# First layer of the third last token group by seven products too, weight sums in the q and k staging tiles, sums added in place in PSUM

## The chip, the cores and the metric

The kernel runs on one core of a Trainium2 chip. The metric is the device time of one execution in microseconds. A profiled execution also gives its span, from its first to its last instruction, which is a little shorter than its time. Engines: PE multiplies matrices (PEld loads its weights), DVE and ACT do elementwise work, POOL issues loads and masks, SP issues stores. PSUM has eight banks of 512 fp32 columns; a matmul's result lands in one of them.

## The reference

Causal attention over 8 batches, 8 heads, 576 tokens of 64 dimensions with 16 extra "beacon" keys in front, then a two-layer MLP with a quick gelu on all 4608 tokens:

```python
scores = scale * np.matmul(q, k_all.transpose(0, 1, 3, 2))     # k_all: 16 beacons, then k
scores = np.where(causal, -1000000000.0, scores)
a = np.exp(scores - scores.max(-1, keepdims=True)); a /= a.sum(-1, keepdims=True) + 1e-09
x = np.matmul(a, v_all).transpose(0, 2, 1, 3).reshape(4608, 512)
h = x @ w_in                                                   # 512 x 2048
g = h * (1.0 / (1.0 + np.exp(-1.702 * h)))
return g @ w_out                                               # 2048 x 512
```

## The kernel before

**Attention** goes by 16 sets (a batch and four heads each). For a set, q and k are loaded into staging tiles (qn, kn, three of each, set s in number s % 3), transposed by DVE (L435), multiplied into score chunks (`qk0` to `qk54`, L464, shape 32x128), put through exp on ACT (L475) and masked on POOL (L496). DVE adds the columns for the normaliser (`zadd`, L514). The value products (`av`, L551, shape 128x32) have two halves of the normaliser per set (`av14.2.0` is set 14, normaliser, half 0) and three others; DVE turns and inverts the normaliser (`z1`, `z2`: L563, L570, L574) and writes the normed result to xT (`norm`, L586), 512 rows of the MLP's input by 2304 columns that are used in turn.

**The MLP** goes by ten token groups: two of 256 tokens, then eight of 512 (groups 2 to 9). Its weights w1t (first layer) and w2t lie in SBUF in fp16.

*First layer.* In groups 0 to 7 it is direct (L610): 16 tiles of 128 features, four 128x512 products each, then a gelu on ACT (L631). In groups 8 and 9 (`FAST`, L752) it uses seven products in place of eight on 2x2 blocks (Strassen and Winograd). Four sums of weight quarters are made once by DVE (`e_ws`, L755), four sums of token quarters per group (`e_xs`, L778). Then come four tiles, i = 0 to 3, of seven products each (L813); each product is four 128x256 matmuls. The sums of products are built in PSUM, in four banks a, b, e, f per tile: product 1 goes to a; ACT copies a to b (`seedb`, L823); product 2 is added in a, and ACT takes the gelu of a; product 6 is added in b, and ACT copies b to e (`seede`); product 7 goes to f, and ACT copies it to SBUF (`keep7`, L828). Product 5 is added in e; DVE adds the kept product 7 to it and writes the sum to SBUF (`sum22`, L831), and ACT takes the gelu from there. Product 3 is then added in e, for a third gelu. Product 4 is added in b; DVE adds product 7 (`sum21`), again into SBUF, for the fourth gelu (L837). The weight sums lie in a tile of the E pool (which otherwise holds exp's results) and in bkf, the token sums in another tile of that pool, and the kept and summed tiles in all six q and k staging tiles.

*Second layer.* Groups 2 to 9 use seven products as well (`products`, L1056; L724 on PE): DVE makes 16 sums of gelu results per group (`s`, L675), and a chain of one ACT copy (`half`, L735) and seven DVE joins (`join`, L740) builds four output quarters, which SP stores (L747).

**Order.** Every engine's order is written out: `ORDER` lists operation numbers, in the order in which the program makes the operations. `Plan.run` goes through these lists with planned durations to fix in which PSUM bank each tile opens and in what order instructions are emitted. Four lower banks (`ring`) are free for tiles all the time. The four upper banks hold the score chunk until the last exp, and from then on any tile may open there. A seeded tile (b or e) may only open in a bank that was fully written before and is closed. A bank is closed by the last reader named in `closers`: a by its gelu, f by `keep7`, b by `sum21`, e by its last gelu; a value tile by its z1 or norms; a product tile of the second layer by its half or join.

PE's list from the last but one score chunk to the first product of group 8, with names for numbers (`m1.7.6`: group 7, feature tile 6; `m2.6.5.4`: second layer of group 6, product 5, from feature tile 4; `f8.0.1`: group 8, tile 0, product 1):

```
qk53 m2.6.4.2 m2.6.7.4 m2.6.7.6 m2.6.5.0 m2.6.5.2 m2.6.4.4 qk54 m1.7.6 m2.6.5.4 m2.6.5.6 m2.6.4.6 m1.7.10 m1.7.1
av14.2.1 av14.2.0 m1.7.8 m2.6.3.4 m1.7.2 m1.7.9 m2.6.3.6 m1.7.13 m1.7.14 m1.7.15 m1.7.0 m1.7.3 m1.7.11 m1.7.4
m1.7.7 m2.7.5.0 m1.7.5 m1.7.12 av14.1.1 av15.2.1 av15.2.0 av14.0.0 av14.0.1 (16 of group 7's second layer)
av15.1.1 av15.0.0 av15.0.1 m2.7.2.6 f8.0.1
```

The lines that the change touches are those of `Plan.run` (L150), `ring_tile`, `e_qk`, L752 to L842, and `fast` and the loops behind it in the kernel's last third. The functions:

Of the kernel before, what the change touches and what calls it, by code (L numbers as in the profile page):

```python
# [32 lines left out]
        978, 1000, 992, 982, 974, 998, 990, 984, 988, 980, 1002, 986, 1256, 1156, 1113, 1111, 1115, 1159, 1025, 1020,  # L33
        1026, 1021, 1259, 1022, 1027, 1023, 1031, 1028, 1032, 1265, 1164, 1162, 1166, 1033, 1034, 1287, 1036, 1041,
        1054, 1055, 1037, 1289, 1042, 1038, 1039, 1047, 1048, 1043, 1292, 1192, 1049, 1050, 1044, 1180, 1170, 1275,
        1278, 1172, 1056, 1176, 1174, 1057, 1190, 1196, 1198, 1168, 1178, 1182, 1184, 1194, 1243, 1186, 1188, 1285,
        1301, 1304, 1281, 1283, 1227, 1237, 1244, 1216, 1238, 1217, 1218, 1221, 1232, 1245, 1222, 1219, 1223, 1228,
        1246, 1311, 1307, 1309, 1224, 1321, 1233, 1229, 1337, 1230, 1234, 1239, 1235, 1325, 1240, 1323, 1327, 1329,
        1341, 1330, 1339, 1343, 1333, 1250, 1251, 1353, 1252, 1346, 1253, 1345, 1359, 1422, 1357, 1355, 1369, 1349,
        1406, 1412, 1401, 1402, 1361, 1423, 1362, 1413, 1365, 1417, 1407, 1371, 1373, 1418, 1375, 1408, 1377, 1414,  # L40
        1403, 1378, 1428, 1381, 1429, 1451, 1445, 1404, 1409, 1419, 1415, 1467, 1461, 1447, 1430, 1431, 1465, 1424,
        1449, 1435, 1463, 1436, 1470, 1469, 1437, 1454, 1420, 1453, 1473, 1499, 1493, 1425, 1438, 1457, 1477, 1497,
        1546, 1495, 1479, 1481, 1483, 1502, 1501, 1485, 1552, 1536, 1547, 1505, 1525, 1526, 1489, 1486, 1541, 1537,
        1527, 1530, 1531, 1548, 1532, 1528, 1538, 1542, 1553, 1549, 1533, 1539, 1543, 1544, 1554, 1555, 1559, 1560,
        1561, 1562,
# [8 lines left out]
        836, 846, 830, 848, 850, 842, 1084, 879, 1087, 1090, 1099, 1097, 1118, 1121, 1147, 1150, 977, 995, 979, 997,  # L54
        993, 973, 975, 983, 991, 999, 989, 1001, 981, 1003, 985, 987, 1257, 1260, 1024, 1266, 1269, 1288, 1290, 1293,
        1181, 1171, 1177, 1175, 1173, 1191, 1179, 1169, 1185, 1197, 1183, 1193, 1195, 1189, 1187, 1199, 1220, 1322,
        1326, 1338, 1324, 1328, 1342, 1340, 1344, 1332, 1336, 1334, 1354, 1360, 1348, 1356, 1352, 1350, 1358, 1364,
        1370, 1366, 1368, 1372, 1374, 1376, 1380, 1382, 1384, 1452, 1405, 1446, 1468, 1462, 1448, 1466, 1464, 1450,
        1476, 1472, 1460, 1474, 1500, 1494, 1456, 1458, 1478, 1498, 1496, 1482, 1484, 1508, 1480, 1506, 1504, 1488,
        1490, 1492, 1529,  # L60
# [13 lines left out]
        945, 941, 943, 1081, 956, 957, 958, 871, 1082, 1094, 1095, 959, 872, 873, 867, 859, 961, 962, 964, 965, 860,  # L74
        863, 1262, 1143, 861, 874, 862, 868, 864, 967, 865, 971, 866, 969, 884, 869, 870, 1101, 1144, 890, 1145,
        1102, 895, 1103, 1104, 900, 906, 1109, 907, 1110, 913, 1106, 1107, 1152, 1153, 1004, 1154, 1005, 1155, 1264,
# [26 lines left out]
    ],  # L103
    "SP": [
        0, 2, 4, 5, 6, 7, 83, 84, 85, 86, 88, 89, 90, 91, 181, 93, 94, 95, 96, 187, 217, 223, 348, 364, 371, 377,
        544, 560, 567, 573, 689, 705, 712, 718, 885, 901, 908, 914, 1030, 1046, 1053, 1059, 1226, 1242, 1249, 1255,
        1411, 1427, 1434, 1440, 1535, 1551, 1558, 1564,
    ],
}
# [1204 lines left out]
```

## Time and profile before

| | |
|---|---|
| median of 3 runs | 326.32 us (326.07 to 326.36) |
| profiled execution, its time | 325.29 us |
| its span | 323.6 us |
| granted PE clock, mean | 0.998 |
| PE waits for others, whole span | 8.4 us, none after 92.1 us |
| first direct product of group 7 | 238.07 us |
| last exp | starts 238.23 us |
| first of the seven products (group 8) | 265.5 us |
| last products on PE | from 317.49 us, 16 of them |

In a row of a timeline stand the start, the length, the engine, line, operation, operands and count; a bracket gives the idle time of the engine before it and what ended that. In a row of groups, the busy time and the mean length of one in ns follow the bar. Lengths of neighbours overlap, since an instruction starts while the one before it is still draining: the distance of two starts is what an engine spends on one. The chain of work that ended last has PE in 83% of the span.

### The profile page before, as it was taken

What the parts mean: (1) busy time and instruction counts of PE and PEld (TensorE: products, weight loads), DVE (VectorE), ACT (ScalarE), POOL (GpSimd) and SP (SyncE); (2) the same over time, 40 slices, a digit from 0 to 9 for tenths busy, and PEclk for the clock granted to TensorE, in tenths of its full rate; (3) what the DMA queues carried; (4) which work ended last, traced back from release to release, by engine and by line L of the source; (5) the groups of instructions that cost most, each with busy time, mean ns of one, the idle gap of its engine ahead of it and who ended that gap; (6) DMA issues with size and microseconds to landing.
All of it is one profiled execution on the core that took longest, in us unless ns stands there. A gap on an engine that the chain in (4) does not pass through costs nothing.

```text
span 323.6 us, 10241 instructions
## 1 busy us (share of the span) xinstructions
PE 310.6 (96%) x4460; PEld 223.6 (69%) x4460; DVE 253.2 (78%) x508; ACT 213.7 (66%) x260; POOL 114.1 (35%) x178
## 2 busy tenths in 40 slices
PE   6589999999999999999999999999999999999994
PEld 6467765544775467745878878647765688888884
DVE  4837788777987989986998879858757788854865
ACT  1685687678767586679757696768664606576840
POOL 8775488190319312951068109500230000000000
PEclk9999999999999999999999999999999999999999
DMA  7999999293424921593019909800100101100203
GB/s 126 162 201 210 206 184 187 48 118 105 104 69 68 180 54 34 67 190 68 2 38 162 158 2 101 180 2 5 34 28 6 67 2 67 65 2 33 100 3 130
DMA packets 58222, 28.85 MB, mean 89 GB/s; under 512 B 41280, under 2 KB 53568, under 8 KB 58176
## 3 DMA queue, kind: packets, MB, share of 16 engines
q0 software_dynamic: 47552, 18.49, 48.3%
q1 hardware_dynamic: 10560, 9.69, 9.2%
q8 instruction: 35, 0.57, 0.7%
q14 instruction: 11, 0.09, 0.1%
q10 hardware_dynamic: 64, 0.01, 0.0%
HBM read 37.22 MB, written 9.44 MB: 144 GB/s over the span
## 4 chain that ended last, share of the span: by engine, by line
PE 83%; DMA 6%; ACT 3%; POOL 3%; DVE 3%; issue 1%; DVEq 0%; ACTq 0%; POOLq 0%
PE u L724 28%; PE u L610 27%; PE u L551 9%; PE s L464 8%; PE u L813 8%; PE u L655 4%; DMA w<-in_moe_w_out_dram 3%; DMA w<-in_moe_w_in_dram 2%; ACT E L475 2%; DVE osb L740 1%; DVE sA L675 1%; POOL vb L395 1%; POOL w L401 0%; ACT L631 0%; POOL kn L379 0%
## 5 line engine op out<-in xcount | busy, mean ns | idle before, releaser
L475 ACT ACTIVATE E<-s 128x2048 f16<-128x2048 f32 (+5 forms) x66 | 98.9, 1515 | 42.6 <-PE s L464 42.1
L610 PE MATMUL u<-xT,w 128*128 128x512 f16 (+1 forms) x576 | 101.9, 332 | 1.1 <-DVE xT L586 0.6
L496 POOL TENSOR_SCALAR_AFFINE_SELECT E<-E 128x512 f16<-128x512 f16 (+3 forms) x78 | 49.5, 666 | 107.4 <-ACT E L475 98.4
L610 PEld LDWEIGHTS <-w 128*128 128x128 f16 x576 | 55.0, 98 | 41.0 <-issue 2.1
L631 ACT ACTIVATE g<-u 128x512 f16<-128x512 f32 x96 | 51.7, 599 | 21.4 <-PE u L610 21.1
L724 PEld LDWEIGHTS <-g 128*128 128x128 f16 x512 | 48.4, 98 | 7.1 <-issue 0.2
L724 PE MATMUL u<-w,g 128*128 128x256 f16 x384 | 50.4, 273 | 0.0
L740 DVE SCALAR_TENSOR_TENSOR osb<-u,osb 128x512 f32<-128x512 f32 x56 | 37.3, 682 | 11.2 <-PE u L724 6.9
L724 PEld LDWEIGHTS <-sA 128*128 128x128 f16 x384 | 36.3, 98 | 6.1 <-issue 0.3
L464 PEld LDWEIGHTS <-kT 32*128 32x128 f16 x1376 | 25.1, 92 | 21.8 <-issue 13.7
L464 PE MATMUL s<-qT,kT 32*128 32x32 f16 (+20 forms) x1376 | 34.3, 228 | 5.2 <-DVE qT L435 2.8
L724 PE MATMUL u<-tB,sA 128*128 128x256 f16 x256 | 35.6, 273 | 0.1
L586 DVE TENSOR_TENSOR xT<-u,rz 128x352 f16<-128x352 f32 (+2 forms) x52 | 25.6, 516 | 7.7 <-PE u L551 7.5
L395 POOL DMA_DIRECT2D vb<-in_v_dram x32 | 27.4, 876 | 2.5 <-DMA qn<-in_q_dram 1.4
L551 PE MATMUL u<-E,vb 128*32 128x352 f16 (+8 forms) x928 | 27.5, 262 | 0.0
L514 DVE TENSOR_TENSOR zs<-zs,E 128x1344 f16<-128x1344 f16 (+2 forms) x36 | 22.3, 619 | 3.1 <-POOL E L496 2.3
L551 PEld LDWEIGHTS <-vb 128*32 128x32 f16 (+1 forms) x928 | 19.9, 96 | 5.4 <-issue 1.7
L675 DVE TENSOR_TENSOR sA<-g 128x512 f16<-128x512 f16 x32 | 13.0, 416 | 13.3 <-ACT g L631 9.9
L435 DVE STREAM_TRANSPOSE kT<-kn 128x576 f32<-128x576 f32 x16 | 20.1, 1258 | 2.1 <-DMA kn<-in_k_dram 1.3
L435 DVE STREAM_TRANSPOSE qT<-qn 128x576 f32<-128x576 f32 x16 | 19.9, 1241 | 0.4 <-DMA qn<-in_q_dram 0.4
L563 DVE STREAM_TRANSPOSE zt<-u 128x224 f32<-128x224 f32 (+2 forms) x32 | 14.9, 469 | 6.1 <-PE u L551 5.9
L514 DVE TENSOR_TENSOR zs<-E 128x1856 f16<-128x1856 f16 x12 | 15.9, 1322 | 3.3 <-POOL E L496 3.3
(70 smaller groups left out, 358.5 us busy)
## 6 DMA issues: line engine op xcount, KB each, us to landing
out_dram<-osb SPq DMA_DIRECT2D x36, 256.0 KB, 2.5
kn<-in_k_dram POOLq DMA_DIRECT2D x16, 288.0 KB, 7.1
qn<-in_q_dram POOLq DMA_DIRECT2D x16, 288.0 KB, 6.9
vb<-in_v_dram POOLq DMA_DIRECT2D x24, 128.0 KB, 6.8
w<-in_moe_w_in_dram POOLq DMA_DIRECT2D x8, 256.0 KB, 9.2
w<-in_moe_w_out_dram POOLq DMA_DIRECT2D x4, 512.0 KB, 13.8
vb<-in_v_dram POOLq DMA_DIRECT2D x8, 112.0 KB, 5.0
vb<-in_v_dram POOLq DMA_DIRECT2D x8, 80.0 KB, 7.8
```

The lines of the kernel that those rows point to most:

```text
L395: nc.gpsimd.dma_start(out=t[0 : hi - lo, j, h0:h1, :], in_=v[b, h0:h1, lo:hi, :].rearrange("h n d -> n h d"),)
L435: nc.vector.transpose(out=f32(dst.rearrange("p n e -> p (n e)")).rearrange("p (r t) -> p t r", t=TR), in_=f32(src[:, :]).rearrange("p (t c ...
L464: nc.tensor.matmul(sc[:, h, o : o + w], kT[s % NB2][r : r + 32, j * P : (j + 1) * P, d], qT[s % NB2][r : r + 32, a : a + w, d], start=(d = ...
L475: nc.scalar.activation(out=Es[s][:, :, c0:c1], in_=ss[i][:, :, o : o + c1 - c0], func=AFT.Exp, scale=0.125,)
L496: nc.gpsimd.affine_select(out=blk, in_=blk, compare_op=ALU.is_ge, fill=0.0, base=off + (Nb if j == 0 else 0), pattern=[[0, Q], [1, w]], ch ...
L514: nc.vector.tensor_tensor(out=t, in0=E[:, :, Z0:S] if i == 1 else t, in1=E[:, :, wcol[i] : wcol[i] + S - a], op=ALU.add,)
L551: nc.tensor.matmul(u[32 * h : 32 * h + 32, a:e], lhs, src[0:kw, h, col : col + e - a], start=first, stop=last,)
L610: nc.tensor.matmul(u[:, o + a - t0 : o + e - t0], w1t[:, kp, nt * P : (nt + 1) * P], xT[:, kp, a % XR : (e - 1) % XR + 1], start=(kp == 0) ...
L631: nc.scalar.activation(out=gts[g][:, n0:n1, 0:w], in_=rings[("m1", g, n0)][:, 0 : n * w].rearrange("p (n w) -> p n w", n=n), func=AFT.Gelu ...
L724: nc.tensor.matmul(u[:, HM * mt : HM * (mt + 1)], lhs[:, n, mt * P : (mt + 1) * P], rhs[:, n, :], start=(n == 0 and mt == 0), stop=(n == H ...
L740: nc.vector.scalar_tensor_tensor(out=osbs[(g, dst)][:, :], in0=rings[("p", g, p)][:, :], scalar=scale_of(g), in1=osbs[(g, src)][:, :], op0 ...
L813: nc.tensor.matmul(u[:, HM * n : HM * (n + 1)], lhs[:, x, (2 * i + n) * P : (2 * i + n + 1) * P], rhs[:, x, :], start=fresh and n == 0 and ...
```

## The change

`FAST` now holds group 7 too, and groups 7 to 9 are numbered behind all of attention. So group 7's first layer is 28 products of four 128x256 matmuls in place of 64 of 128x512, with four token sums, eight seeds, four keeps and eight sums by DVE. In all three groups the DVE sums go to PSUM: `sum22` from bank e into bank f, `sum21` in place in bank b; f is now closed by the gelu that reads it, and b too. Product 7 is kept in qn[0] or kn[0] by turns. The weight sums lie in qn[1], kn[1], qn[2], kn[2], in bkf, and the fourth in place in the quarter of w1t that no other product reads; each is made by two DVE instructions of 1024 columns, one per half. The token sums lie in three tiles of the sig pool and one in place in xT, and are used by all three groups in turn. `Plan.run` takes the earliest of the engines' next operations at each step, and opens tiles in the upper banks for the first layer's seven-product tiles only; all others stay in the lower four. `PHASE` is empty, so there is one break, after the last score chunk.

`ORDER` is new from group 6's first layer on (on DVE two pairs of weight sums come earlier). The same stretch of PE's list:

```
qk53 m2.6.4.0 m2.6.4.2 m2.6.7.4 m2.6.7.6 f7.0.1 m2.6.5.4 qk54 m2.6.4.4 m2.6.4.6 m2.6.5.6 f7.0.2 f7.0.6
m2.6.3.0 m2.6.3.2 m2.6.3.4 m2.6.3.6 f7.0.7 f7.1.1 av14.2.0 f7.0.5 f7.2.1 f7.1.2 f7.0.4 f7.1.6 f7.1.7 av14.2.1
f7.0.3 f7.2.2 f7.1.4 f7.3.1 f7.1.5 f7.2.6 av15.2.0 av14.0.1 av14.1.1 av14.0.0 av15.2.1 f7.1.3 f7.2.7 f7.3.6
f7.3.7 f7.3.2 f7.2.5 f7.3.5 f7.2.4 av15.0.0 av15.0.1 av15.1.1 m2.7.4.0 f7.3.4 f7.3.3 f7.2.3 f8.0.1
```

On ACT `seedb7.0` stands ahead of the last exp; on DVE the weight sums stand behind two sums of group 5, behind a join of group 5, behind `zadd13` and between group 7's token sums.

```diff
+        def opening(o):
+            open_at, ph = [], self.phase.get(o.ring, -1)
+            for i, key in enumerate(bank):
+                if i >= self.ring:
+                    if ph < 0 or ph < spell:
+                        continue
+                    if ph > spell:
+                        key = None
+                if o.ring in self.seeded and (key is None or key in self.partial):
+                    continue
+                ends = [c.end for c in self.closers[key]] if key is not None else []
+                if key is None and i >= self.ring:
+                    ends = [c.end for c in self.late[ph]]
+                if None not in ends:
+                    open_at.append((max([0] + [x + 60 for x in ends]), i))
...
-    FAST = (8, 9)
+    FAST = (7, 8, 9)
+    PHASE = {}
+    plan.breaks = sorted(set(PHASE.values())) + [len(CHUNKS) - 1]
     SF, ST = {}, {}
 
+    def pair(a, b):
+        return [t[:, 0 : DFF // 2] for t in (a, b)]
+
+    SF[1], SF[2] = pair(qn[1], kn[1]), pair(qn[2], kn[2])
+    SF[4] = bkf[:, :, :].rearrange("p a d -> p (a d)").bitcast(F16).rearrange("p (x n) -> p x n", x=2)
+    SF[4] = [SF[4][:, x, :] for x in range(2)]
+
+    def w1q(f, j):
+        return [w1t[:, 2 * j + x, DFF // 2 * f : DFF // 2 * (f + 1)] for x in range(2)]
+
+    SF[3] = w1q(1, 0)
...
     def e_ws(i):
-        if not SF:
-            t = ep.tile([P, Q, ETOT], F16, tag="E", name="E")
-            t = t.rearrange("p a n -> p (a n)")
-            for n, k in enumerate((1, 2, 4)):
-                SF[k] = t[:, 2 * n * DFF // 2 : 2 * (n + 1) * DFF // 2].rearrange("p (x n) -> p x n", x=2)
-            SF[3] = bkf[:, :, :].rearrange("p a d -> p (a d)").bitcast(F16).rearrange("p (x n) -> p x n", x=2)
-        a11, a12, a21, a22 = (
-            w1t[:, 2 * j : 2 * j + 2, DFF // 2 * f : DFF // 2 * (f + 1)] for f in range(2) for j in range(2)
-        )
-        if i == 1:
-            add("DVE", SF[1], a21, a22, ALU.add)
-        elif i == 2:
-            add("DVE", SF[2], SF[1], a11, ALU.subtract)
-        elif i == 3:
-            add("DVE", SF[3], a11, a21, ALU.subtract)
-        else:
-            add("DVE", SF[4], a12, SF[2], ALU.subtract)
+        out, a, b, o = {
+            1: (SF[1], w1q(1, 0), w1q(1, 1), ALU.add),
+            2: (SF[2], SF[1], w1q(0, 0), ALU.subtract),
+            3: (SF[3], w1q(0, 0), w1q(1, 0), ALU.subtract),
+            4: (SF[4], w1q(0, 1), SF[2], ALU.subtract),
+        }[i]
+        for x in range(2):
+            add("DVE", out[x], a[x], b[x], o)
...
     def e_xs(g, i):
-        if g not in ST:
-            if "t" not in SF:
-                SF["t"] = ep.tile([P, Q, ETOT], F16, tag="E", name="E")
-            t = SF["t"].rearrange("p a n -> p (a n)")
-            o = len(ST) * 4 * 2 * HM
-            ST[g] = [
-                t[:, o + n * 2 * HM : o + (n + 1) * 2 * HM].rearrange("p (x n) -> p x n", x=2) for n in range(4)
-            ]
-        t1, t2, t3, t4 = ST[g]
+        if not ST:
+            for n in (1, 2, 4):
+                t = sp.tile([P, 512], F16, tag="sig", name="sig")
+                ST[n] = t[:, :].rearrange("p (x n) -> p x n", x=2)
         b11, b12, b21, b22 = (tokens(g, j, h) for j in range(2) for h in range(2))
         if i == 1:
-            add("DVE", t1, b12, b11, ALU.subtract)
+            add("DVE", ST[1], b12, b11, ALU.subtract)
         elif i == 2:
-            add("DVE", t2, b22, t1, ALU.subtract)
+            add("DVE", ST[2], b22, ST[1], ALU.subtract)
         elif i == 3:
-            add("DVE", t3, b22, b12, ALU.subtract)
+            add("DVE", b12, b22, b12, ALU.subtract)
         else:
-            add("DVE", t4, b21, t2, ALU.subtract)
+            add("DVE", ST[4], b21, ST[2], ALU.subtract)
 
...
-        xt = ST.get(g, [None] * 4)
-        wq = lambda f, j: w1t[:, 2 * j : 2 * j + 2, DFF // 2 * f : DFF // 2 * (f + 1)]
         lhs, rhs = {
-            1: (wq(0, 0), tokens(g, 0, 0)),
-            2: (wq(0, 1), tokens(g, 1, 0)),
-            3: (SF.get(4), tokens(g, 1, 1)),
-            4: (wq(1, 1), xt[3]),
-            5: (SF.get(1), xt[0]),
-            6: (SF.get(2), xt[1]),
-            7: (SF.get(3), xt[2]),
+            1: (w1q(0, 0), tokens(g, 0, 0)),
+            2: (w1q(0, 1), tokens(g, 1, 0)),
+            3: (SF[4], tokens(g, 1, 1)),
+            4: (w1q(1, 1), ST.get(4)),
+            5: (SF[1], ST.get(1)),
+            6: (SF[2], ST.get(2)),
+            7: (SF[3], tokens(g, 0, 1)),
...
-    hold = [f32(t[:, 0 : 2 * 512]) for t in qn + kn]
-
-    def e_keep7(src, slot):
-        nc.scalar.mul(out=hold[slot], in_=rings[src][:, :], mul=1.0)
-
-    def e_sum7(src, slot, dst):
-        nc.vector.tensor_tensor(out=hold[dst], in0=rings[src][:, :], in1=hold[slot], op=ALU.add)
+    p7s = {}
+
+    def e_keep7(g, i, src, slot):
+        if slot is None:
+            p7s[(g, i)] = os.tile([P, DMODEL], F32, tag="osb", name="osb")[:, :]
+        else:
+            p7s[(g, i)] = f32((qn[0], kn[0])[slot][:, 0 : 2 * 512])
+        nc.scalar.mul(out=p7s[(g, i)], in_=rings[src][:, :], mul=1.0)
+
+    def e_sum7(g, i, src, dst):
+        nc.vector.tensor_tensor(out=rings[dst][:, :], in0=rings[src][:, :], in1=p7s[(g, i)], op=ALU.add)
...
-            in_=(hold[src] if isinstance(src, int) else rings[src][:, :]).rearrange("p (n w) -> p n w", n=2),
+            in_=rings[src][:, :].rearrange("p (n w) -> p n w", n=2),
...
-            free = [avs[(NSET - 3, x, 1)] for x in range(2)] + [bkc[NSET - 1]]
+            both = lambda s: [turn[(s, 0)], turn[(s, 1)]]
+            free = {
+                1: both(NSET - 3), 2: both(NSET - 2), 4: [bkc[NSET - 1]],
+                3: [x for n in range(g) for x in m1s[n]],
+            }
             prev = None
             for i in (1, 2, 4, 3):
-                prev = wsum[i] = op("DVE", 1200, free + [prev], lambda i=i: e_ws(i), name="wsum")
-        free = [avs[(NSET - 2, x, 1)] for x in range(2)]
+                prev = wsum[i] = op("DVE", 1250, free[i] + [prev], lambda i=i: e_ws(i), name="wsum")
+        free = readers.get(g - 1, [])
         xsum, prev = {}, None
...
         def tiles(i):
             key = {x: ("f", x, g, i) for x in "abef"}
+            for x in key.values():
+                plan.phase[x] = ph
             plan.seeded.update((key["b"], key["e"]))
-            turns15 = [turn[(s, w)] for s in range(NSET - NB3, NSET) for w in range(2)]
             k = len(held)
-            slots = [3 * (k % 2) + x for x in range(3)]
-            last = held.get(k - 2, turns15)
+            slot = k % 2 if fixed else None
+            last = []
+            if fixed:
+                last = held.get(k - 2) or [turn[(NSET - 1, w)] for w in range(2)]
...
-                return op(
+                o = op(
                     "PE", 2 * SQ * 109, deps, lambda: e_part(g, p, i, key[at], fresh), kind="m1",
                     ring=key[at], mode="m", name=f"f{g}.{i}.{p}",
...
             p1 = part(1, "a", [], True)
             c1 = grab("seedb", 490, [p1], lambda: e_seed(key["a"], key["b"]), ring=key["b"])
             p2 = part(2, "a", [c1])
-            gelu(0, 0, p2, key["a"], key["a"])
+            gelu(0, 0, p2, "a")
             p6 = part(6, "b", [c1])
             c2 = grab("seede", 490, [p6], lambda: e_seed(key["b"], key["e"]), ring=key["e"])
             p7 = part(7, "f", [], True)
-            x7 = grab("keep7.", 480, [p7] + last, lambda: e_keep7(key["f"], slots[0]), closes=key["f"])
+            x7 = grab("keep7.", 480, [p7] + last, lambda: e_keep7(g, i, key["f"], slot))
             p5 = part(5, "e", [c2])
             p4 = part(4, "b", [c2])
-            a1 = grab("sum22.", 605, [p5, x7] + last, lambda: e_sum7(key["e"], slots[0], slots[1]), "DVE")
-            g22 = gelu(1, 1, a1, slots[1])
+            a1 = grab("sum22.", 605, [p5, x7], lambda: e_sum7(g, i, key["e"], key["f"]), "DVE")
+            gelu(1, 1, a1, "f")
             p3 = part(3, "e", [a1])
-            gelu(0, 1, p3, key["e"], key["e"])
-            a2 = grab("sum21.", 605, [p4, x7] + last, lambda: e_sum7(key["b"], slots[0], slots[2]), "DVE", closes=key["b"])
-            g21 = gelu(1, 0, a2, slots[2])
-            held[k] = [a1, a2, g22, g21]
+            gelu(0, 1, p3, "e")
+            a2 = grab("sum21.", 605, [p4, x7], lambda: e_sum7(g, i, key["b"], key["b"]), "DVE")
+            gelu(1, 0, a2, "b")
+            held[k] = [a1, a2]
...
-                while s % HS == HS - 1 and g < NG and GROUPS[g][1] <= (s // HS + 1) * S:
+                while s % HS == HS - 1 and g < FAST[0] and GROUPS[g][1] <= (s // HS + 1) * S:
                     mlp(g)
                     g += 1
+    for g in FAST:
+        mlp(g)
+
...
-    plan.late = [x for n in range(len(CHUNKS[-1])) for x in [exps[(len(CHUNKS) - 1, n)]]]
+    for ph, i in enumerate(plan.breaks):
+        plan.late.append([exps[(i, n)] for n in range(len(CHUNKS[i]))])
+        if i + 1 < len(CHUNKS):
+            for o in closing[ph]:
+                also(qks[i + 1], o)
```

## The prediction

> **What bounds the kernel.** I read the first two parts of the page, then the busy time by stretch.
>
> ```profile
> PE 310.6 (96%) x4460; PEld 223.6 (69%) x4460; DVE 253.2 (78%) x508; ACT 213.7 (66%) x260; POOL 114.1 (35%) x178
> PE   6589999999999999999999999999999999999994
> ...
> 220.00:238.00 18.00, 18.00 (x384) 14.16 (x382) 14.10 (x32) 12.70 (x11) 3.35 (x5) 1.00 0.05 17
> 238.00:258.00 20.00, 20.00 (x207) 11.17 (x194) 14.21 (x27) 11.74 (x18) 3.06 (x4) 1.00 0.12 41
> 258.00:266.00 8.00, 8.00 (x117) 6.80 (x115) 7.18 (x19) 0.60 (x1) 0.00 (x0) 1.00 0.01 2
> ```
>
> The columns of the last three are the stretch, its length, the busy time of PE, weight load, DVE, ACT and POOL, then the granted clock. PE is full in each, at clock 1.00. A busy PE need not be a PE at its peak, so I laid the planned order of PE end to end from the score chunk that the timeline shows at 220.66, with spacings of this trace: 0.4365 us for four 128x256 products, 0.866 for four 128x512, 0.58 for a score chunk, 0.09 for a change of array shape, the value products by their columns. The sum ends at 319.38; in the trace the last 16 products start at 317.49 and four groups later it is 319.24. The 0.14 between is rounding of my spacings, on the side of no wait: PE waits for nothing in those 99 us, and what it does there sets the end.
>
> **What goes and comes on PE.** The PE timeline:
>
> ```profile
> 245.91 7.07 PE L610 MATMUL u<-xT,w 128*128 128x512 f16 x32
> 252.81 0.60 PE L724 MATMUL u<-tB,sA 128*128 128x256 f16 x4
> ...
> 281.25 0.60 PE L724 MATMUL u<-tB,g 128*128 128x256 f16 x4
> ...
> 289.98 1.47 PE L724 MATMUL u<-w,g 128*128 128x256 f16 x12
> ```
>
> Columns: start, length, engine, line, operands, count. 32 products of 512 columns take 252.81 - 245.91 = 6.90 us. All 64 of group 7 lie between 238.07 and 255.07; with the six groups of four and the two value products taken out, 13.83 us are left. From 281.25 to 289.98, with L813 and L724 mixed, stand 20 groups of four: 0.4365 each. The new group 7 has 4 tiles x 7 products x one such group: 28 x 0.4365 = 12.22 us. Saved: 13.83 - 12.22 = 1.61 us. The count of weight loads rises from 64 to 112, at 98 ns each (L813), under a spacing of 109 ns: the rate just used already holds them. The order splits the two normaliser products of set 14, which stood together, into two visits: one more change of shape, 0.09 (group before the chunk at 237.48 ends at 236.95 + 0.4365 = 237.39). **On PE: -1.52 us**, and the same end-to-end sum over the new order is 317.83, 1.55 earlier. I take -1.5.
>
> **What the other engines get.** These rows give prices:
>
> ```profile
> L831 DVE TENSOR_TENSOR qn<-u,qn 128x512 f32<-128x512 f32 x8 | 5.5, 687 | 1.0 <-ACT qn L828 0.9
> L823 ACT ACTIVATE u<-u 128x512 f32<-128x512 f32 x16 | 9.4, 589 | 7.8 <-DVE osb L740 5.3 <-PE u L813 2.3
> L828 ACT ACTIVATE qn<-u 128x512 f32<-128x512 f32 x4 | 2.4, 597 | 1.3 <-PE u L813 1.3
> L837 ACT ACTIVATE g<-qn 128x512 f16<-128x512 f32 x8 | 4.9, 628 | 2.4 <-DVE qn L831 2.3
> L837 ACT ACTIVATE g<-u 128x512 f16<-128x512 f32 x16 | 9.5, 592 | 3.1 <-PE u L813 2.3 <-DVE g L675 0.7
> ```
>
> The mean is a single one's length; two in a row of the sum cover 1.29, so the next starts 0.60 behind; two ACT copies cover 1.14, so 0.55 at most. Group 7 brings ACT 8 seeds and 4 keeps, 12 x 0.55 = 6.6 us, with as many gelus as before. ACT idles 8.3 us in 238 to 258 and 7.4 in 258 to 266: hidden. The eight gelus of held sums in each of groups 8 and 9 read PSUM instead: 36 ns less each, 0.6 us in all, nothing on the path. DVE gets 8 sums x 0.60 = 4.8 us and four token sums of 0.34 = 1.4. Against it stands the move of the weight sums: four of 1.22 us lay at 244, 248, 252 and 262.6, that is 4.9 us out of the very stretch that the new sums enter. As eight halves they cost 0.68 each (0.42 at 512 columns, 1.22 at 2048, so 0.52 ns a column), 5.4 us in all. Three pairs go to these gaps, whose idle time stands in brackets:
>
> ```profile
> 187.36 0.76 DVE L675 TENSOR_TENSOR sA<-g 128x512 f16<-128x512 f16 x2 [1.68 <-ACT g L631]
> 203.09 0.95 DVE L514 TENSOR_TENSOR zs<-zs,E 128x832 f16<-128x832 f16 x2 [0.66 <-POOL E L496]
> 215.35 0.43 DVE L675 TENSOR_TENSOR sA<-g 128x512 f16<-128x512 f16 x1 [3.90 <-ACT g L631]
> 240.45 1.29 DVE L740 SCALAR_TENSOR_TENSOR osb<-u,osb 128x512 f32<-128x512 f32 x2 [3.49 <-PE u L724]
> ```
>
> 1.3 us into 1.68; 1.3 into 0.66 and the 0.38 just behind it, so that some 0.3 is late for z of set 12, whose users come only after group 6's 14 us; 1.3 into 3.90. The fourth pair and group 7's token sums, 2.7 us, come between 231 and 237, ahead of the 3.49. Without these covers the 2.7 us would push the first join behind them and, with it, the bank that the first seed needs. No DMA is issued, moved or dropped by any of it.
>
> **Where PE could now wait.** Dense 512-column work needed only xT; the seven products hang on ACT and DVE by turns. I followed the new order by hand with those rows. The first product starts at 236.18, ahead of the last score chunk (237.14). Its seed needs a written bank that is closed, the one that group 6's join of product 7 leaves at 237.2, and ends at 237.8; the last exp goes from there to 239.7, the table load to 240.95, then gelu, seed 2 until 241.95, keep until 242.9. The fifth product is at 242.76: 0.8 spare. Tile 1's second product stands at 243.64, its seed ends at 243.4: 0.2 spare, and 0.2 to 0.3 for the next two seeds. While one of these waits, ACT's gelus of older tiles queue behind it, and the bank that they close. The third product of tile 0 at 245.68 wants the sum in PSUM, 244.3: 1.4 spare. The thinnest are bank hand-overs, because value and second-layer tiles now use the lower four banks alone: at 223.2, 248.5 to 249.4 (three) and 310.4 (the bank that half 9 leaves at 310.35) I find 0.0 to 0.2 spare. Groups 8 and 9 have 0.4 to 1.1. My hand-overs carry 0.1 either way, so I find no wait over 0.1 and book nothing, with up to 1.4 us (five at 0.25, plus 0.1) in the range.
>
> **The sum into PSUM** is the one price without a row: no DVE instruction here writes PSUM. Bound below by the same sum into SBUF, 0.69; above by twice that, 1.37, as if source and destination took turns. ACT's copy into PSUM against SBUF (589 to 597 ns) says that the destination hardly matters; I take 0.69. [...] No run here shows a DVE write to PSUM so far.
>
> **The tail.**
>
> ```profile
> 315.56 4.77 DVE L740 SCALAR_TENSOR_TENSOR osb<-u,osb 128x512 f32<-128x512 f32 x7 [1.97 <-issue]
> 317.49 1.91 PE L724 MATMUL u<-w,sA 128*128 128x256 f16 x16
> ```
>
> Seven joins run packed, 0.68 apart, to 320.33, 0.93 behind PE. In the new order two joins can end before the last six groups of PE, and five follow from 315.4: done at 318.85, 0.95 behind the new end of PE (319.40 - 1.5 = 317.9). The tail stays: 3.3 us for the last store.
>
> **Sum:** span 323.6 - 1.5 = 322.1. The execution profiled took 325.29, 1.7 outside the span, and the median of the runs is 1.03 above it; both are carried unchanged: 326.32 - 1.5 = 324.8.
>
> **Rivals.**
> - *The four lower banks hold PE back.* For it: the five thin places; in the plan before, these tiles could use all eight banks after the last exp. Against: the hops in the trace (an ACT copy's recorded end to the next PE start) leave no gap anywhere in the 99 us. Five waits of 0.25 give 1.25: 326.1, no change; 325.3 to 326.5 for half and for a bit more. This is also how the change would do nothing for the time.
> - *Slower: the sums into PSUM make DVE the bound.* Place: DVE's queue from 243 to 258, where the value rows of sets 14 and 15 (norm, zt) stand behind the sums. At 1.37 a sum, eight are 5.4 us late, of which idle DVE takes about 2.5 and the 2 us ahead of group 8's first product take more: PE waits about 1; in groups 8 and 9 two sums are 1.4 late against 0.9 to 1.1 spare, some six times 0.3: 1.8. Total -1.5 + 2.8 = +1.3: 327.6. It starts to tell at about 0.25 us more a sum and reaches the old time near 0.5. Against it: ACT's two rows.
> - *The chain through ACT is late once a tile.* 0.2 spare turned into 0.2 late at four seeds is 0.8: 325.6; it lies within the first case's upper edge.
>
> **Chances.** No wait or small ones, 324.2 to 325.6: 0.71. Banks: 0.19. DVE: 0.10. What can be told from no change is 0.2%, 0.65 us, so faster means under 325.67: all but 0.03 of the first case and a third of the second, 0.74; slower over 326.97: 0.09; the rest 0.17. Range 324.2 (the tail gains 0.6 as well) to 326.2 (the banks take nearly all).
>
> **What will show it.** Right: group 7's products in groups of four at 0.4365, the last score chunk near 237.1, PE without idle from 92 us on, last matmul near 317.9. The sums show a PSUM destination with their length. Wrong: PE waits on ACT between 242 and 250, or on DVE at 223, 249 or 310; a sum near 1 us; or the PE end unmoved with no idle named, which would mean that the spacing is not 0.4365 when weights come from the staging tiles.

## The result, and the profile after

The changed kernel takes 325.17 us (median of 9 runs, 324.49 to 325.97), the kernel before beside it 326.17 (9 runs, 325.72 to 326.38): a ratio of 0.9968 [0.9957, 0.9979], 1.0 us less (0.7 to 1.4). Two later comparisons gave 0.9947 [0.9934, 0.9959] and 0.9965 [0.9952, 0.9977]. So it is a little faster, as forecast, by 0.3 to 0.5%; 1.0 to 1.7 us was measured where 1.5 was said.

The execution profiled took 324.84 us, its span is 323.1 (before: 325.29 and 323.6). Line numbers have moved: scores are L484, exp L495, masks L516, `zadd` L534, value products L571, z1 L583, sums of `add` L695, second layer L744, join L760, seven products L831, seeds L841, `keep7` L850, the sums into PSUM L853. From the first two parts of the page of the changed kernel:

```profile
PE 312.2 (97%) x4508; PEld 230.0 (71%) x4508; DVE 261.7 (81%) x524; ACT 219.5 (68%) x272; POOL 113.4 (35%) x178
...
PE   7689999999999999999999999999999999999994
```

Its busy time by stretch, with the columns of the prediction:

```profile
220.00:238.00 18.00, 18.00 (x353) 13.59 (x350) 16.17 (x38) 13.43 (x12) 2.98 (x5) 1.00 0.05 17
238.00:258.00 20.00, 20.00 (x317) 16.57 (x316) 18.61 (x37) 16.40 (x28) 2.56 (x5) 1.00 0.12 42
258.00:266.00 8.00, 8.00 (x76) 7.18 (x74) 7.59 (x22) 3.21 (x6) 0.00 (x0) 1.00 0.09 33
```

PE is as full as before, with more and shorter products. DVE is what has changed: 18.61 + 7.59 = 26.2 of the 28 us from 238 to 266, where it had 14.21 + 7.18 = 21.4. 1.8 us are left to it there.

The waits of PE over the whole span, in us in total, times, and the longest:

```profile
PE s L484 <- ACT E L495: 2.0, 4, 0.9
PE u L1326 <- DVE tB L311: 1.9, 1, 1.9
PE s L484 <- DVE qT L455: 1.6, 2, 1.4
PE u L630 <- ACT g L651: 0.5, 1, 0.5
PE u L571 <- DVE E L509: 0.2, 1, 0.2
```

None of them is on a seed (L841), a keep (L850), a sum into PSUM (L853) or a join: all lie in the first third of the span, before any of the new work.

**Where the gain sits.** Because PE waits for nothing late in the span, I compared starts: the same instruction in two traces, and how far apart they are. Score chunks 47 to 49 stand in the same places of both orders, and the last products of the second layer end both.

| start of, us | before | after | after minus before | step |
|---|---|---|---|---|
| score chunk 12 | 45.27 | 46.04 | +0.77 | |
| score chunk 47 | 202.76 | 203.55 | +0.79 | +0.02 |
| score chunk 48 | 205.56 | 206.58 | +1.02 | +0.23 |
| score chunk 49 | 220.66 | 221.69 | +1.03 | +0.01 |
| last 12 products of PE | 317.93 | 317.59 | -0.34 | -1.37 |

The last row of PE in the trace of the changed kernel is

```profile
317.59 1.47 PE L744 MATMUL u<-w,sA 128*128 128x256 f16 x12
```

(Before, the last row holds 16 products from 317.49; four products later it is 317.49 + 0.4365 = 317.93.) Behind chunk 49 both traces hold the same products, but for group 7's first layer. Three things are to be seen. The new stretch gains **1.37 us**. At chunk 48 **0.23 us** are given back. And this execution was 0.77 us late by chunk 12 already, before anything that the change touches; the first execution profiled of the kernel before was an early one, which its time says too (325.29 against a median of 326.32). The difference of the two spans, 0.5 us, is therefore no measure of the change.

### The profile page after: what moved, and what is told of

Read it like the earlier page. It is cut to its first block, busy times and chain, and to the rows that moved or that the text cites. A ratio compares the mean times of both kernels' runs of the same rounds, so it can differ in the third digit from the quotient of the medians.

```text
span 323.1 us, 10371 instructions
## 1 busy us (share of the span) xinstructions
PE 312.2 (97%) x4508; PEld 230.0 (71%) x4508; DVE 261.7 (81%) x524; ACT 219.5 (68%) x272; POOL 113.4 (35%) x178
## 5 line engine op out<-in xcount | busy, mean ns | idle before, releaser
L495 ACT ACTIVATE E<-s 128x2048 f16<-128x2048 f32 (+5 forms) x66 | 98.9, 1515 | 41.4 <-PE s L484 40.9
L630 PE MATMUL u<-xT,w 128*128 128x256 f16 (+1 forms) x512 | 87.3, 326 | 0.6 <-ACT g L651 0.5
L516 POOL TENSOR_SCALAR_AFFINE_SELECT E<-E 128x512 f16<-128x512 f16 (+3 forms) x78 | 48.8, 658 | 107.5 <-ACT E L495 94.2
L630 PEld LDWEIGHTS <-w 128*128 128x128 f16 x512 | 49.0, 98 | 34.7 <-issue 1.9
L651 ACT ACTIVATE g<-u 128x512 f16<-128x512 f32 x80 | 43.2, 599 | 15.6 <-PE u L630 15.4
L744 PEld LDWEIGHTS <-g 128*128 128x128 f16 x512 | 48.5, 98 | 7.1 <-issue 0.3
L744 PE MATMUL u<-w,g 128*128 128x256 f16 x384 | 49.9, 273 | 0.0
L760 DVE SCALAR_TENSOR_TENSOR osb<-u,osb 128x512 f32<-128x512 f32 x56 | 37.6, 683 | 13.6 <-PE u L744 11.7
L484 PEld LDWEIGHTS <-kT 32*128 32x128 f16 x1376 | 25.6, 93 | 20.6 <-issue 12.1
L744 PEld LDWEIGHTS <-sA 128*128 128x128 f16 x384 | 36.3, 98 | 5.1 <-issue 0.3
L484 PE MATMUL s<-qT,kT 32*128 32x32 f16 (+20 forms) x1376 | 34.9, 230 | 3.9 <-ACT E L495 2.0
L859 ACT ACTIVATE g<-u 128x512 f16<-128x512 f32 x48 | 26.9, 602 | 12.4 <-PE u L831 6.8
L744 PE MATMUL u<-tB,sA 128*128 128x256 f16 x256 | 34.9, 273 | 0.1
L571 PE MATMUL u<-E,vb 128*32 128x352 f16 (+8 forms) x928 | 27.9, 265 | 0.0
L534 DVE TENSOR_TENSOR zs<-zs,E 128x1344 f16<-128x1344 f16 (+2 forms) x36 | 22.6, 628 | 2.3 <-POOL E L516 1.6
L571 PEld LDWEIGHTS <-vb 128*32 128x32 f16 (+1 forms) x928 | 19.8, 97 | 5.5 <-issue 1.5
L831 PE MATMUL u<-xT,w 128*128 128x256 f16 x144 | 20.5, 273 | 0.0
L831 PEld LDWEIGHTS <-w 128*128 128x128 f16 x192 | 18.8, 98 | 2.2
```

Source lines behind the costliest of these rows:

```text
L484: nc.tensor.matmul(sc[:, h, o : o + w], kT[s % NB2][r : r + 32, j * P : (j + 1) * P, d], qT[s % NB2][r : r + 32, a : a + w, d], start=(d = ...
L495: nc.scalar.activation(out=Es[s][:, :, c0:c1], in_=ss[i][:, :, o : o + c1 - c0], func=AFT.Exp, scale=0.125,)
L516: nc.gpsimd.affine_select(out=blk, in_=blk, compare_op=ALU.is_ge, fill=0.0, base=off + (Nb if j == 0 else 0), pattern=[[0, Q], [1, w]], ch ...
L571: nc.tensor.matmul(u[32 * h : 32 * h + 32, a:e], lhs, src[0:kw, h, col : col + e - a], start=first, stop=last,)
L630: nc.tensor.matmul(u[:, o + a - t0 : o + e - t0], w1t[:, kp, nt * P : (nt + 1) * P], xT[:, kp, a % XR : (e - 1) % XR + 1], start=(kp == 0) ...
L651: nc.scalar.activation(out=gts[g][:, n0:n1, 0:w], in_=rings[("m1", g, n0)][:, 0 : n * w].rearrange("p (n w) -> p n w", n=n), func=AFT.Gelu ...
```

## The experiments

**The same programs once more.** To see how much of the 0.77 belongs to the execution, the unchanged code of both kernels was profiled again.

> The changed kernel once more, with a profile of its own, beside the kernel before on the same chip. Theory: the 0.77 us by which its first profile was late at score chunk 12 (46.04 against 45.27 us) belongs to that execution, since both programs have the same instructions, banks and waits on PE up to group 6's first layer; here the chunk starts anywhere from 45.0 to 46.3, while from chunk 47 to chunk 48 there are again 3.03 us (2.80 before) and from chunk 49 to the start of the last 12 products 95.9 us. Time 0.9 to 1.3 us under the kernel before. Rival: the late start belongs to the changed kernel; then chunk 12 is at 46.0 or later again, and a gain of 1.5 is worth only 0.5 to 0.9.

> The kernel before, unchanged, with a profile of its own. Theory: the start of its first profile was an early one (that execution took 325.29 us, 1.03 under the median), so here score chunk 12 begins later than 45.27 us, at 45.7 to 46.4 like the three profiles of changed kernels (46.04, 46.12, 46.31), while chunk 49 to the start of the last 12 products of PE stays at 97.3 us. Time level. Rival: the changed kernel starts later by itself; then chunk 12 is at 45.1 to 45.4 once more.

> The changed kernel a third time, as the measure for the two beside it: 0.9 to 1.7 us under the kernel before, chunk 12 of its profile anywhere from 45.2 to 46.7 us.

Measured: the changed kernel 324.81 us against 326.48 (0.9947 [0.9934, 0.9959]) and 325.02 against 326.24 (0.9965 [0.9952, 0.9977]); the kernel before, run as its own competitor, 326.28 against 326.35 (0.9998 [0.9988, 1.0007]). The second profile of the kernel before took 326.73 us with a span of 325.0, and its chunk 12 starts at 46.69, 1.42 later than in its first profile and past the 46.4 that was expected. The two later profiles of the changed kernel have it at 46.12 and 46.59. From chunk 49 to the last 12 products the two profiles of the kernel before have 97.27 us each, and the three of the changed kernel 95.90, 95.91 and 95.90. So the start varies by execution and the stretch does not: in each pair of profiles the 1.37 is there, to 0.01. By time the changed kernel was 1.67 us ahead on the one chip, more than the 0.9 to 1.3 expected, and 1.22 on the other.

**The second pair of weight sums moved.** At chunk 48 the trace of the changed kernel shows what is late. DVE:

```profile
202.54 0.68 DVE L760 SCALAR_TENSOR_TENSOR osb<-u,osb 128x512 f32<-128x512 f32 x1
203.13 0.68 DVE L695 TENSOR_TENSOR qn<-qn,w 128x1024 f16<-128x1024 f16 x1
203.74 1.11 DVE L695 TENSOR_TENSOR kn<-kn,w 128x1024 f16<-128x1024 f16 x1
204.77 0.94 DVE L534 TENSOR_TENSOR zs<-zs,E 128x832 f16<-128x832 f16 x2
```

Before, the sums of the last row (`zadd` of set 12) began at 203.09; with the 0.79 by which this execution is late that is 203.88, and they began at 204.77, 0.9 late. PE in the changed kernel reads them right ahead of chunk 48:

```profile
205.98 0.62 PE L571 MATMUL u<-zs,ones 128*32 128x352 f16 x8
206.41 0.24 PE L571 MATMUL u<-E,ones 128*32 128x80 f16 x8
206.58 0.66 PE L484 MATMUL s<-qT,kT 32*128 32x256 f16 x32
```

The eight products on the sums take 0.43 from start to start; before they took 0.21 (205.19 to 205.40). There is no idle time in brackets: a wait of 0.43 - 0.21 = 0.22 lies inside the recorded length, 0.62 us here and 0.38 before. The edit that tests this moves step 1226 of DVE's list, the second pair, to stand with the third:

```diff
+def move(engine, what, before):
+    seq = ORDER[engine]
+    seq.remove(what)
+    seq.insert(seq.index(before), what)
+
+move("DVE", 1226, 1227)
```

> The second pair of weight sums on DVE moves from ahead of the last two normaliser sums of set 12 to just ahead of the third pair, into the idle time behind set 13's second normaliser sum. Theory: chunk 48 follows chunk 47 by 2.80 us again, as before the change, the later turns of set 15 are not felt, and the time falls by 0.23 us against the changed kernel (ratio to before 0.996). Rival: the 0.23 belongs to the execution or to the new order elsewhere: 3.03 us stay, and the time is unchanged; or the turns of set 15, 1.3 us later, make chunk 51 wait.

Measured: 324.85 us, 0.9947 [0.9933, 0.9960], beside 324.81 for the unmoved kernel on the same chip: the 0.23 expected does not show in the time. The trace tells the two apart. PE and DVE of this kernel (lines are 8 further down):

```profile
206.26 0.38 PE L579 MATMUL u<-zs,ones 128*32 128x352 f16 x8
206.47 0.23 PE L579 MATMUL u<-E,ones 128*32 128x80 f16 x8
206.62 0.66 PE L492 MATMUL s<-qT,kT 32*128 32x256 f16 x32
```

```profile
212.44 0.68 DVE L703 TENSOR_TENSOR qn<-qn,w 128x1024 f16<-128x1024 f16 x1
213.04 0.68 DVE L703 TENSOR_TENSOR kn<-kn,w 128x1024 f16<-128x1024 f16 x1
```

The eight products are back at 0.21, and from chunk 47 to 48 it is 2.79 us, as in the kernel before (2.80), where all six profiles of kernels with the pair in its place of the changed order have 3.03 to 3.05. The two halves take 0.68 each where they stand now. So the pair cost 0.23 to 0.26 us at chunk 48 and nothing at its new place, the 95.91 behind it being unchanged.

**The two visits of set 14 in one as well.** On top of it, the second normaliser product of set 14 is put right behind the first, and value and second-layer tiles may use all eight banks again (the edit of the next experiment, which by itself changes nothing):

```diff
+move("DVE", 1226, 1227)
+move("PE", 1187, 1241)
...
-            open_at, ph = [], self.phase.get(o.ring, -1)
+            open_at, ph = [], self.phase.get(o.ring, 0)
...
```

> As pair2_later, and the two normaliser products of set 14 stand next to each other on PE again; for that, tiles of all kinds may open in the upper four banks after the last exp, as before the change. Theory: an own visit of PE to the other array shape costs 0.16 us (0.09 going in and some 0.07 coming out, by the starts of this profile), so the stretch from chunk 49 to the last 12 products falls by 0.16 and the time by 0.4 against the changed kernel in all. Rival of the banks: with eight banks for all tiles it gains clearly more than 0.4, since PE waited for banks; or the visit costs nothing and it gains 0.23 only.

> pair2_one_visit once more, on a chip with the changed kernel: 0.23 us from the weight sums and 0.13 from the visit, together 0.36, so 0.1 to 0.6 us under the changed kernel by the medians. Rival: its first gain of 0.3 was chance, and it is level.

Measured: 324.5 us against 326.48, 0.9939 [0.9926, 0.9953], and on another chip 324.6 against 326.24, 0.9952 [0.9937, 0.9966], where the changed kernel as it is had 325.02. From chunk 49 to the last 12 products it is 95.81 in both, 0.10 less than without, where 0.16 and 0.13 were expected. This version has the lowest medians of all that ran, ahead of the changed kernel by 0.3 and 0.4 us, of which the traces account for 0.23 + 0.10. A visit of its own, in the trace of the changed kernel:

```profile
245.97 0.60 PE L831 MATMUL u<-xT,w 128*128 128x256 f16 x4
246.50 0.33 PE L571 MATMUL u<-zs,ones 128*32 128x352 f16 x4
246.77 0.61 PE L831 MATMUL u<-xT,bkf 128*128 128x256 f16 x4
```

245.97 to 246.50 is 0.53 for four products that take 0.4365 among their kind: the 0.09 of a change of shape, which the prediction booked once for this visit. But a visit also costs on its way out. The same 16 matmuls of set 14's normaliser stand in one visit before; after, 12 of them stand in a first visit and the four above in a second:

```profile
242.07 0.38 PE L551 MATMUL u<-zs,ones 128*32 128x352 f16 x8
242.28 0.23 PE L551 MATMUL u<-E,ones 128*32 128x80 f16 x8
242.44 1.04 PE L610 MATMUL u<-xT,w 128*128 128x512 f16 x4
```

```profile
243.56 0.23 PE L571 MATMUL u<-zs,ones 128*32 128x112 f16 x4
243.62 0.23 PE L571 MATMUL u<-E,ones 128*32 128x80 f16 x8
243.78 0.28 PE L831 MATMUL u<-sig,qn 128*128 128x256 f16 x1
```

Before, they take 0.37 (242.07 to 242.44); after, 0.22 (243.56 to 243.78) and 0.27 (246.50 to 246.77), 0.12 more. So the extra visit costs 0.09 + 0.12 = 0.21 us, and the second profile of each kernel has the same. Only 0.10 came back because the merged kernel has two short waits, 0.13 in all, that the changed kernel doesn't have:

```profile
246.04 0.60 PE L840 MATMUL u<-xT,bkf 128*128 128x256 f16 x4
246.56 0.60 PE L840 MATMUL u<-xT,w 128*128 128x256 f16 x4
247.04 0.60 PE L840 MATMUL u<-sig,w 128*128 128x256 f16 x4
```

```profile
245.90 1.09 ACT L850 ACTIVATE u<-u 128x512 f32<-128x512 f32 x2
```

0.52 and 0.48 stand where four products take 0.4365. The two seeds in this row of ACT end at 246.51 and at 245.90 + 1.09 = 246.99, and the products that need them start 0.05 later each; by these times, it is the seeds that PE waits for.

**All banks, the first rival of the prediction.** If the four lower banks held PE back, giving value and second-layer tiles the upper four again after the last exp would free it:

```diff
-            open_at, ph = [], self.phase.get(o.ring, -1)
+            open_at, ph = [], self.phase.get(o.ring, 0)
...
```

> The changed kernel with one thing undone: after the last exp, value tiles and second-layer tiles may open in the upper four banks too, as before the change; order and work are the same. Theory: no bank hand-over holds PE in the changed kernel, since its starts from chunk 49 to the end follow the sum of its work to 0.13 us; so 95.9 us from chunk 49 to the start of the last 12 products again, and the time within 0.2 us of the changed kernel. Rival (the banks of the prediction): up to 1.2 us faster.

Measured: 325.12 us, 0.9964 [0.9952, 0.9976], beside 325.02 for the changed kernel on the same chip. From chunk 49 on, 95.91 against 95.90. The banks cost nothing; the rival is out.

**Group 7 direct again, all else new.** Is the gain that of the products alone, or does the rest of the new order bring some? `FAST` is set back, and the order is the old one up to group 8's first product and the new one from there, with all eight banks open after the last exp as in the experiment above:

```diff
...
-    FAST = (7, 8, 9)
+    FAST = (8, 9)
...
```

> Group 7's first layer is direct again, with everything else of the change kept: sums into PSUM, weight sums in the staging tiles and in place, token sums shared by groups 8 and 9. Engines go by the old order up to the first product of group 8, by the new one from there, and all eight banks are open to all tiles after the last exp. Theory: the gain is the PE work of group 7's products alone, so this is level with the kernel before: 0.0 us, from -0.3 to +0.5 (the join of two orders may cost a wait). Rival: part of the gain comes from the other parts (shorter gelus, sums in PSUM, a better order behind group 8): then it is 0.5 us or more under the kernel before.

Measured: 330.91 us, 1.0141 [1.0119, 1.0164], 4.4 us slower than the kernel before, where level was expected; this does not answer the question. Its waits of PE are headed by

```profile
PE u L738 <- ACT u L748: 3.4, 3, 2.5
```

L738 are the products and L748 the seeds of group 8: where the two lists meet, seeds come later on ACT than the products need them. So the entries behind the seam were put in another order, in which the seeds come earlier on ACT; nothing else was changed:

> As direct7_rest_new, with the order of PE, ACT and DVE shifted behind the join of the two orders so that the seeds of group 8 are made earlier than PE wants them. Theory: the 4.4 us that direct7_rest_new lost were PE's waits at the join (3.6 us, 3.4 of them on seeds) and its span's late start; without them it is level with the kernel before, -0.3 to +0.4 us. Rival: some of the changed kernel's gain lies in the other parts of the change: 0.5 us or more under the kernel before.

Measured: 326.38 us, 1.0000 [0.9989, 1.0010]. This kernel has the sums into PSUM for groups 8 and 9, the weight sums in the staging tiles and all eight banks open, and it takes the time of the kernel before. Its list of waits of PE has none after the first third, but its stretch from chunk 49 is 97.65 us, against 97.27 before. The 0.38 are two waits too short for the list, 0.27 and 0.12 more than the products take among their kind:

```profile
300.85 0.60 PE L651 MATMUL u<-tB,sA 128*128 128x256 f16 x4
301.56 1.15 PE L738 MATMUL u<-xT,w 128*128 128x256 f16 x8
302.55 0.27 PE L738 MATMUL u<-sig,qn 128*128 128x256 f16 x1
```

Without them it would be 97.26, as before. So the parts of the change other than group 7's products gain nothing that the trace shows: the gain is theirs.

**Dearer sums, the second rival.** The price that this rival needs did not come (the sums take 0.69 us, see below). To see whether the rival was sized rightly, each sum into PSUM got company: one more sum of 192 columns (or two of 256) ahead of it, into an SBUF tile that nothing reads, so that what the kernel computes stays as it is. For 192 columns:

```diff
+    waste = cst.tile([P, 256], F32, tag="waste", name="waste")
...
+        for _ in range(1):
+            nc.vector.tensor_tensor(
+                out=waste[:, 0:192], in0=rings[src][:, 0:192], in1=p7s[(g, i)][:, 0:192], op=ALU.add
+            )
```

> Ahead of each of the 24 sums into PSUM, DVE also adds 192 columns of the same operands into an SBUF tile that nobody reads: 0.26 us more a sum, by 0.69 us for 512 columns. This is where the prediction put the point from which a slower sum tells. Theory: no or little loss against the changed kernel, 0.0 to 0.4 us. Rival: DVE is already the bound between 238 and 266 us, where the profile shows it busy for 26.2 of 28 us; then eight sums of group 7 bring their 2 us whole, or most of it.

> Ahead of each of the 24 sums into PSUM, DVE also adds the same operands in two halves of 256 columns into an SBUF tile that nobody reads: 0.65 us more a sum, near the upper bound that the prediction had for the sum. Theory, from the prediction's DVE rival (2.8 us at 0.68 us more): 1.8 to 3.2 us over the changed kernel, PE waiting between 245 and 262 us for sums and for value rows behind them, and in groups 8 and 9 by about 0.3 at a sum. Rival: the 1.4 us to spare at a tile's third product take it all: under 0.5 us.

Measured: 326.33 us, 1.0001 [0.9990, 1.0012], with one more sum of 192 columns, and 335.92, 1.0293 [1.0276, 1.0309], with two of 256, both beside 326.35 for the kernel before on that chip. Both are far more than was expected. DVE's busy time is 267.9 and 279.1 us, against 261.7 in the changed kernel: over 24 sums 0.26 and 0.73 more for each. A quarter of a microsecond on each of 24 DVE instructions takes the whole gain away. The stretch from chunk 49 is 97.47 us with the first (1.57 more than without) and 107.04 with the second (11.1 more). Busy time of the first of the two by stretch:

```profile
238.00:258.00 20.00, 19.66 (x310) 16.19 (x299) 19.49 (x43) 15.39 (x25) 2.27 (x4) 1.00 0.12 41
258.00:266.00 8.00, 8.00 (x76) 7.17 (x74) 7.82 (x21) 4.23 (x8) 0.00 (x0) 1.00 0.08 26
```

and PE's waits in the second, those on the work around the sums:

```profile
PE u L832 <- DVE u L858: 1.4, 3, 0.5
...
PE u L572 <- ACT g L864: 1.2, 2, 0.8
PE u L745 <- DVE g L696: 1.1, 1, 1.1
PE u L832 <- DVE zt L584: 1.1, 1, 1.1
PE u L745 <- DVE sA L696: 0.8, 2, 0.4
PE u L745 <- DVE osb L761: 0.5, 1, 0.5
PE u L745 <- DVE xT L607: 0.5, 1, 0.5
PE u L832 <- ACT u L842: 0.5, 1, 0.5
```

DVE has 27.3 of 28 us from 238 to 266 in the first: it is the bound, or all but. In the second the list gives PE only 1.4 us of waits for the sums themselves (L858), and more for what stands in DVE's queue behind them: the value rows (zt, xT), sums of gelus (g, sA), joins (osb), and by way of a join's bank the seeds (L842). In the first, PE loses 1.57 us, of which the row of 238 to 258 shows 0.34 as idle (20.00 - 19.66); laid beside the changed kernel product by product, 0.87 of it grows up to 257 us and the other 0.70 in steps of 0.08 to 0.21 between 275 and 302, at products of groups 8 and 9 and of the second layer. In the second, 4.75 of the 11.1 us are lost by 265 us and 6.4 behind that.

## Why the prediction was right, and where it was not

- **PE's share** was said to be -1.52 and is -1.37. The new order laid end to end came out at 317.83 for the end, from a chunk at 220.66; moved to the same chunk, the trace has 317.59 + 3 x 0.4365 - 1.03 = 317.87. That sum was right to 0.04. What was off is the difference of the two sums, since that over the old order had come out 0.14 long; this was noted and then left in. In the count by products, 0.03 is that 64 x 6.90 / 32 is 13.80 and not 13.83. The term that was mis-sized is the extra visit to the other array shape: 0.09 was booked for it, the change of shape on the way in, and it costs 0.21, since the way out takes 0.12 more (see the experiment on set 14). These two make up the 0.15. None of it is a wait: in the stretch from 238 to 256 the groups of four follow each other at 0.4365 to within 0.01 us, and only changes of shape add to that.
- **The sum into PSUM**, the price without a row, was taken at 0.69 of 0.69 to 1.37. It is 0.69 to 0.70:

```profile
L853 DVE TENSOR_TENSOR u<-u,kn 128x512 f32<-128x512 f32 x12 | 8.2, 693 | 3.4 <-PE u L831 1.8 <-ACT kn L850 1.6
L853 DVE TENSOR_TENSOR u<-u,qn 128x512 f32<-128x512 f32 x12 | 8.2, 696 | 2.2 <-PE u L831 1.9 <-ACT g L859 0.2
```

  That is 6 to 9 ns over the 687 of the same sum into SBUF.
- **The weight sums.** The step that failed is "1.3 into 0.66 and the 0.38 just behind it, so that some 0.3 is late for z of set 12, whose users come only after group 6's 14 us". The pair took 203.13 to 204.77, 1.64 us, not 1.3, and what was late first was not z but the `zadd` ahead of it, whose users are the normaliser products in front of chunk 48. I had followed the value rows forward from z and not asked who reads the instruction that the pair was put in front of. Cost: 0.23 us on PE. The first and third pairs and the fourth were hidden as said; the idle time of 1.68 ahead of `sA` in group 5 is down to

```profile
188.15 0.76 DVE L695 TENSOR_TENSOR sA<-g 128x512 f16<-128x512 f16 x2 [0.47 <-ACT g L651]
```

- **The chain through ACT** held. The first seed waited for the bank that the join of group 6 leaves, as was said, and PE's list had other work:

```profile
238.52 0.58 ACT L841 ACTIVATE u<-u 128x512 f32<-128x512 f32 x1 [1.15 <-DVE osb L760]
```

- **The banks** (chance 0.19): no cost, and none given back when the banks were opened.
- **DVE as the bound** (0.10) did not come, since the price stayed low, but the rival was much too mild: it was to "start to tell" at 0.25 us more a sum, reach the old time near 0.5 and cost 2.8 us at 0.68: 1 in group 7 and 1.8 in groups 8 and 9. On the chip the old time is reached at 0.26, and 0.73 costs 11.1. Two of its terms were mis-sized. For group 7 it is the idle time that DVE has to swallow the delay. The prediction put it at about 2.5 us, and 2 more ahead of group 8's first product; the new order leaves 1.8 in all. I had gone by the old trace (21.4 of 28 us busy), put the eight new sums against the four weight sums that leave, and stopped there. By operation, from 238 to 266, the weight sums did take 4.8 us out and the sums put 5.5 in (summed lengths; neighbours overlap, so the items here come to more than the 4.8 by which DVE's busy time grew); but two more joins (1.3 us), two more norms (1.0), two more `zadd` (1.2) and four more token sums (1.6) came in besides, since the new order packs more of its neighbours' work into the stretch. Eight sums with 0.26 more are 2.1 us, and 1.8 was left. For groups 8 and 9 it is the 0.9 to 1.1 us said to be spare at two sums: 0.26 more on each sum costs 0.7 us there already, and 0.73 more costs 6.4 and not 1.8. What takes up that spare time stays open.
- **The tail** was to stay: from the end of PE's last products to the end of the span it was 323.6 - 319.24 = 4.4 us, and is 323.1 - 318.90 = 4.2.
- **The sum** put -1.5 on the median. In the traces it is -1.37 + 0.23 = -1.14, 0.2 us more at most with the tail; the three comparisons by time gave -1.0, -1.7 and -1.2.

## What to carry to other kernels

When the engine that sets the end never waits, read a change from the distance between two instructions that both orders share; a difference of two spans holds the start of each execution too, here up to 1.6 us. Work put into another engine's gap has to be followed to the first reader of the instruction that it is put in front of, however early in that instruction's chain. Here a visit to the other array shape cost PE 0.09 us on the way in and 0.12 on the way out, so split visits have to be priced at both ends. And count the slack of the engine next in line in the new order, with all that is pulled forward into the stretch, not in the old trace.

## What the runs showed of the hardware

**The start of an execution varies, and the clock granted to PE goes with it in part at most.** From 14 to 20 us, the kernel before in its first profile and in its second:

```profile
14.00:20.00 6.00, 4.52 (x132) 3.62 (x132) 3.42 (x10) 3.92 (x4) 3.90 (x6) 1.00 1.52 188
```

```profile
14.00:20.00 6.00, 5.39 (x100) 3.76 (x103) 3.56 (x10) 3.04 (x3) 2.63 (x4) 0.50 1.52 189
```

The same program at clock 1.00 does 132 matmuls there in 4.52 us, and at 0.50 only 100 in 5.39; it is 1.42 us later at chunk 12. But with 0.72 in that stretch chunk 12 started at 45.88 to 46.12 in four profiles, with 0.50 at 46.38 to 46.69 in three, and with 1.00 anywhere from 45.27 to 46.84 in six. So the clock is not shown to be the cause of all of it, and no run here isolates it. Early and late starts occur with either kernel: 45.27 and 46.69 before, 45.73 to 46.84 in the changed kernel and its variants.

**A weight-sum half on DVE and two masks on POOL took longer side by side.** The half that took 1.11 us (203.74 to 204.85) ran beside the masks (202.72 to 204.30). These masks in the changed kernel and, with the pair moved, beside a join that ends at 203.50 and an idle DVE from there to 204.18:

```profile
202.72 1.58 POOL L516 TENSOR_SCALAR_AFFINE_SELECT E<-E 128x320 f16<-128x320 f16 x2
```

```profile
203.03 1.11 POOL L524 TENSOR_SCALAR_AFFINE_SELECT E<-E 128x320 f16<-128x320 f16 x2
```

Both sides lost: DVE 0.43 (1.11 against 0.68), POOL 0.47. In all six profiles with the pair beside them the masks take 1.57 or 1.58, and in all three with it moved 1.11 or 1.12. What held them up, and which of the two at which moment, no run here shows: the first half (203.13 to 203.81), beside the same masks, took its 0.68.

**Short waits of PE left no idle time.** A 128x256 product is recorded at 0.27 us and the next one starts 0.11 later, so the first 0.16 us of a wait lie inside its recorded length. The 0.22 us at chunk 48, the 0.13 of the merged visit, the 0.38 of the kernel with group 7 direct and most of the 1.57 us of the kernel with dearer sums are in no list of waits; they are seen only as longer distances between starts.
